# Attention of sorted blocks and a feed-forward layer: transposes on the DMA queues or on TensorE, and a product that gives x^T directly

## The chip, the cores and the metric

The kernel runs on one core of one Trainium2 chip. The metric is the device time of one execution in microseconds (us), as the median of several runs. The engines are TensorE (PE, with its weight loads as PEld), VectorE (DVE), ScalarE (ACT), GpSimd (POOL) and SyncE (SP), which here only issues transfers; POOL issues the loads. Each engine takes its instructions in order, and engines wait for each other by semaphores.

## The reference, cut to what matters

```python
q, k, v: (4, 8, 768, 64)   sort_net: (4, 8, 8, 8)   block = 96
P = sort_net                                    # Sinkhorn, 5 rounds
for _ in range(5):
    P = exp(P - max(P)); P = P / sum(P, -1); P = P / sum(P, -2)
k_sorted = einsum('bhij,bhjcd->bhicd', P, k in 8 blocks of 96)
v_sorted = einsum('bhij,bhjcd->bhicd', P, v in 8 blocks of 96)
scores = (q @ k_sorted^T) / 8                   # inside each block of 96
attn = exp(scores - max); attn = attn / sum(attn, -1)
x = attn @ v_sorted                             # to (3072 tokens, 512)
out = relu(x @ w_in) ** 2 @ w_out               # 512 -> 2048 -> 512, float32
```

## The kernel before

**Work.** The four batches are b = 0 to 3. A *unit* is a pair of heads (hp = 0 to 3) of one batch; a *half* (hf) is four of its eight blocks, 384 positions. The feed-forward layer is worked in eight FFN units of 384 tokens: unit g belongs to batch g // 2, half g % 2. An FFN unit needs `xT` (attention's result, features on partitions) of all four head pairs of its half. It is 16 *ups* (four matmuls of 384 columns each, L997), each followed by a ReLU on ACT (L1005) and a square on DVE (L1008), and then three tiles of 128 tokens in four *down* quarters each (four matmuls of 512 columns, L1027); a tile's result is copied by ACT and written out by SP.

**Attention of one unit.** k and v are sorted: blocks are mixed with weights from P. Batch 0 does it with `w_all` (P times a mask, `s_sort`, L613, and `s_sort2`, L649), which leaves k^T and v^T; `s_vt` (L733) turns v back. Later batches load k and v with four rows of a block in one partition row and sort them with the small `w_t` in 32x32 parts of the array (`s_nat`, L769), which leaves them untransposed; v goes out to HBM and back to come block by block (`v_way`, `vblk`). Two units of batch 1 sort k by `s_sort`. `s_q` (L563) turns q on PE for those and for batch 0. The other ten units take `s_turn`: natural k (`kn`) and a paired copy of q (`qi`, made by DVE, L841) are each turned by a transposing transfer issued by SP, and DVE puts k^T in block order (L829). `s_sc` makes the scores (L684) and ACT their exponentials `et`. In `s_av` a matmul with `et` stationary and v moving (65 columns, the last of ones) gives x and the sums (L875); DVE takes reciprocals of the sums (96x8, L885) and multiplies (L886) into `ao`. `s_xt` turns `ao` into `xT`: by a transposing transfer for eleven whole units and three single halves of batch 0, and by PE (L928) for the rest.

**Buffers.** Scores, later sorts and `attn v` share two PSUM buffers `p2` (ring `r2`). Ups and downs share three (`pf`, ring `rf`), the ReLUs' outputs `h1` have three, output tiles four. `ps1` has one.

**Order.** Everything is first entered in a `Plan`: each operation with an engine, a price in us, what it depends on. FFN work and attention work are two queues for PE; `DUES` says after how many FFN pieces an attention stage is due, and `FIRST` gives the order of the first batch's first halves. `Plan.run` plays this through with its prices and emits each engine's instructions in the resulting order, which is fixed from then on; where PE would have idled early, `fill` puts matmuls with `ones`. Loads of batches 2 and 3 wait for a POOL copy (`held`) that reads `xT` of the batch before; a gate on POOL holds one load of batch 1 back.

Of the kernel before, what the change touches and what calls it, by code (L numbers as in the profile page):

```python
# [11 lines left out]
ALU = mybir.AluOpType  # L12
# [9 lines left out]
    (0, "K"): (-265.0, -237.0, -495.0, -419.0),  # L22
    (0, "S"): (-232.5, -234.0, -349.0, -310.0),
    (0, "T"): (-184.0, -236.0, -400.0, -291.5),
    (0, "A"): (-135.0, -150.0, -300.0, -111.0),
    (0, "X"): (-58.0, -109.0, -251.5, -80.5),
    (0, "W"): (-267.0,),
    (1, "V"): (-117.0, -62.5),
    (1, "Q"): (-58.5,),
    (1, "N"): (None, -31.0),  # L30
    (1, "Z"): (None, None, 2.5, 48.5),
    (1, "S"): (-45.5, -5.0, 5.0, 50.0),
    (1, "A"): (-27.0, -4.5, 31.5, 51.5),
    (1, "X"): (40.0, 23.5, 37.0, 53.5),
    (2, "L"): (40.0,),
    (2, "N"): (75.5, 79.0),
    (2, "V"): (60.5, 82.5),
    (2, "Z"): (81.0, 82.5, 94.0, 83.5),
    (2, "S"): (86.0, 86.5, 96.0, 93.5),
    (2, "A"): (86.0, 88.0, 99.0, 94.5),  # L40
    (2, "X"): (97.5, 103.0, 103.0, 102.0),
    (3, "L"): (109.0,),
    (3, "N"): (111.5, 130.0),
    (3, "V"): (112.5, 144.0),
    (3, "Z"): (128.5, 139.0, 153.0, 149.0),
    (3, "S"): (144.0, 153.0, 158.0, 153.5),
    (3, "A"): (145.0, 153.5, 159.5, 154.5),
    (3, "X"): (150.5, 170.0, 236.5, 211.5),
# [4 lines left out]
FIRST = ("K0' v0 K1 v1 S0 t0' S1 t1' A0 K2' V2 A1 K3 S2 t2 v3 S3 x1' A2 T3' x0' A3 X2' F0 F1 F3 "  # L53
         "F4 F6 F7 X3")
# [130 lines left out]
def kernel(  # L185
# [48 lines left out]
    rkx, rkn, rqi, rqz = Ring(3), Ring(4), Ring(4), Ring(6)  # L234
# [43 lines left out]
    kvT_r, et_r, vs_r, qz_r = [], [], [], []  # L278
    for n in range(3):
        sT = const.tile([128, 2, S + 32], BF16, name=f"kvT{n}")  # L280
        for x in (HS, S):
            nc.vector.memset(sT[:, :, x:x + 32], 0.0)
        kvT_r.append(sT)
        qz = const.tile([128, 2, NA, 128], BF16, name=f"qz{n}")
        qz_r.append(qz)
        vs = (qz.rearrange("p h a x -> p (h a x)")[0:96, 0:NB * 2 * 66]
              .rearrange("p (n h x) -> p n h x", n=NB, h=2))
        nc.vector.memset(vs[:, :, :, D:D + 1], 1.0)
        vs_r.append(vs)
# [11 lines left out]
    kn_r = [const.tile([128, NA, 2, D], BF16, name=f"kn{n}") for n in range(4)]  # L301
    qi_r = [const.tile([128, NA, 2, D], BF16, name=f"qi{n}") for n in range(4)]
    kx_r = []
    for n in range(3):
        kx_r.append(const.tile([128, 128 * NA], BF16, name=f"kx{n}"))
# [8 lines left out]
    w_all = const.tile([128, H + HP, NB, C0], BF16)  # L314
# [22 lines left out]
    def in_tiles(b, t, h0):  # L337
        return b > 1 and t > 0 or b == 1 and t == 2 or b == 1 and t == 1 and h0 == HP
# [44 lines left out]
    def loads_after(deps):  # L383
# [5 lines left out]
        def gate(e):  # L389
            nc.gpsimd.tensor_copy(out=xT[0:1, 0:HP - 1, HS:HS + 1],  # L390
                                  in_=w_out_bf[0:1, NT // 2 - HP + 1:NT // 2, 0:1])

        for t, g in ((2, 0), (2, 1), (1, 0), (0, 0), (1, 1), (0, 1)):
            if t == 0 and g == 1:
                holds["gate"] = plan.add("POOL", 0.1, gate, [landed["w_out", 1]])
                deps = [holds["gate"]]
            load(1, t, HP * g, HP, deps=deps)
            if t == 2 and g == 1:
                landed["last"] = plan.add("DMA", 1.5, lambda e: None, [landed["last"]])
# [131 lines left out]
    class Unit:  # L531


        def __init__(self, b, hp, halves):
            self.b, self.hp, self.halves = b, hp, halves
            self.tiled = in_tiles(b, 1, HP * (hp // 2))
            self.n, self.old = rks.take()
            if self.tiled:
                self.ksT = kvT_r[self.n][:, 0, :]
                self.i0, self.ni, self.full = 0, NB, True  # L540
                return
# [126 lines left out]
    def s_sc(u, due=0):  # L668
# [3 lines left out]
        for hf in u.halves:  # L672
# [4 lines left out]
            def mm(e, hf=hf, st=st, slot=slot):  # L677
                st["p"] = scp = p2[slot]
                if not u.tiled:
                    qT = (tiles["qT", u.b, u.hp].rearrange("p a x -> p (a x)")  # L680
                          .rearrange("p (i q) -> p i q", q=BLK))
                for n in range(NQ):
                    for h in range(2):
# [3 lines left out]
                            rhs=(q_late(u.qz)[64 * h:64 * (h + 1), :,  # L687
                                              C0 * (NQ * hf + n):C0 * (NQ * hf + n + 1)]
                                 if u.tiled else qT[64 * h:64 * (h + 1), NQ * hf + n, :]),
# [5 lines left out]
            if u.tiled:  # L695
                rqz.use(u.qz, pe)
            else:
                rqT.use(qTs[u.b, u.hp], pe)
# [52 lines left out]
    k_nat = {}  # L751

    def s_nat(b, g, t, due):

        if t == 2:
            m, oldm = rvn.take()
        evs = []
        for hp in (2 * g, 2 * g + 1):
            slot, old = r2.take()
            if t == 1:  # L760
                m, oldm = rkn.take()
# [13 lines left out]
            def ev(e, hp=hp, slot=slot, m=m):  # L775
                dst = (vn_r[m][:, :, 2 * (hp % 2):2 * (hp % 2) + 2, 0:D] if t == 2
                       else kn_r[m])
                copy(e, dst, p2[slot][:, :, 0:NA * D].rearrange("p e (a d) -> p a e d", d=D))
# [7 lines left out]
            if t == 1:  # L786
                rkn.use(m, op)
                k_nat[b, hp] = m, op
        if t == 1:
            return  # L790

# [22 lines left out]
    def q_late(z):  # L814
        return qz_r[z % 3][:, z // 3, :, :]

    def s_turn(u):

        b, hp = u.b, u.hp
        m, op = k_nat[b, hp]  # L820
        kx, oldx = rkx.take()

        def k_turn(e):
            nc.sync.dma_start_transpose(
                out=kx_r[kx].rearrange("p (a x) -> p a x", a=NA),
                in_=kn_r[m].rearrange("p a e d -> p (a e d)"))

        def k_blocks(e):
            nc.vector.tensor_copy(out=u.ksT[:, 0:S].rearrange("p (n x) -> p n x", n=NB),  # L829
                                  in_=kx_r[kx].rearrange("p (x n) -> p n x", n=NB))  # L830

        sp = plan.add("SP", 1.4, k_turn, [op, loaded(b)] + oldx)
        k_op = plan.add("WAY", 1.3, lambda e: None, [sp])
        rkn.use(m, k_op)
        u.k_op = plan.add("DVE", 0.87, k_blocks, [k_op] + u.old)
        rkx.use(kx, k_op, u.k_op)

        n, oldi = rqi.take()

        def q_pair(e):  # L840
            nc.vector.tensor_copy(  # L841
                out=qi_r[n].rearrange("p a e d -> p e a d"),
                in_=qkv[b][0][:, 2 * hp:2 * hp + 2, :].rearrange("p e (a d) -> p e a d", d=D))

        qp = plan.add("DVE", 0.4, q_pair, [landed[b, 0, HP * (2 * hp // HP), 0]] + oldi)
        readers[b].append(qp)
        rqi.use(n, qp)
        u.qz, oldz = rqz.take()

        def q_turn(e):  # L850
            nc.sync.dma_start_transpose(
                out=q_late(u.qz), in_=qi_r[n].rearrange("p a e d -> p (a e d)"))

        sp = plan.add("SP", 1.4, q_turn, [qp, loaded(b)] + oldz + [op for ops in rvs.all for op in ops])
# [350 lines left out]
```

## Time and profile before

| what | value |
|---|---|
| median of 3 runs (lowest, highest) | 217.92 us (217.73, 217.99) |
| profiled execution, its own time | 217.95 us |
| span of the profiled execution | 216.2 us |
| PE busy | 209.8 us (97%) |
| DVE, ACT, POOL busy | 109.2, 122.1, 28.3 us |
| granted PE clock | 1.00 |
| ups and downs on PE (L997, L1027) | 506 and 352 matmuls recorded |
| transposing transfers (`xT<-ao`, `kx<-kn`, `qz<-qi`) | 14, 10, 10; median 3.6, 3.9, 3.6 us to landing |
| DMA queues, share of 16 engines | q1 (SP) 40.1%, q0 (POOL) 36.9% |

The span runs from the first to the last instruction; the rest of the execution's own time lies around it. A row such as `L885 DVE RECIPROCAL rec<-p 96x8 f32<-96x8 f32 x32 | busy, mean ns | idle before` names a line of the kernel, its engine and operation, the tiles written and read with partitions x elements, how many there were, their time in all and each, and how long the engine sat idle just before them and for whom. The chain that ended last is followed back from the last instruction, at each step to what released it. Matmuls are pipelined, so a mean of one is longer than the distance from one start to the next.

### The profile page before, as it was taken

The page shows a single profiled execution, that of the slowest core. Times are in us where ns is not written, and L with a number is a line of the kernel's source. Part 1 is how long each engine was busy: PE and PEld are TensorE (multiplying, and loading weights), DVE is VectorE, ACT ScalarE, POOL GpSimd, SP SyncE. Part 2 cuts the span into 40 slices and gives each one's busy share as a digit, 9 for nine tenths or more (in the row PEclk, how much of TensorE's full clock was granted, in tenths as well). Part 3 has the DMA queues.
Part 4 walks back from the last instruction along what each step waited for, and adds up shares of the span by engine and source line. Part 5 has one row for each costly group of instructions (what it writes and reads, how often), then busy time and mean ns, then how long its engine had stood idle before and what let it go on. Part 6 is the DMA issues. An engine that isn't in the chain of part 4 may idle for free.

```text
span 216.2 us, 5062 instructions
## 1 busy us (share of the span) xinstructions
PE 209.8 (97%) x2020; PEld 115.9 (54%) x2036; DVE 109.2 (51%) x297; ACT 122.1 (56%) x251; POOL 28.3 (13%) x53
## 2 busy tenths in 40 slices
PE   8998999999999999999999999999999999999994
PEld 2566675446654565445655455445655465455542
DVE  5777677146795446345875047407775154015300
ACT  4876985248765277347774178318874375137421
POOL 7896230000000700000000420000000000000000
PEclk9999999999999999999999999999999999999999
DMA  6999999999978599199995699497978410120012
GB/s 152 212 203 207 207 207 209 193 226 272 176 164 113 84 238 211 25 192 210 179 186 125 105 201 213 87 207 171 170 204 111 102 47 3 49 97 0 0 52 97
DMA packets 47864, 31.92 MB, mean 148 GB/s; under 512 B 27296, under 2 KB 42912, under 8 KB 47840
## 3 DMA queue, kind: packets, MB, share of 16 engines
q1 hardware_dynamic: 35616, 18.35, 40.1%
q0 software_dynamic: 12224, 13.24, 36.9%
q8 instruction: 16, 0.26, 0.5%
q14 instruction: 8, 0.07, 0.1%
HBM read 29.70 MB, written 8.72 MB: 178 GB/s over the span
## 4 chain that ended last, share of the span: by engine, by line
PE 93%; DVE 2%; ACT 2%; issue 1%; DVEq 0%
PE hp L997 37%; PE op L1027 36%; PE p L875 4%; PE p L440 4%; PE p L684 3%; PE p L769 2%; PE op L1055 2%; PE qtp L563 2%; DVE ao L886 1%; PE vbp L733 1%; PE p L649 1%; DVE h L1008 1%; ACT h L1005 1%; PE xtp L928 1%; PE hp L955 0%
## 5 line engine op out<-in xcount | busy, mean ns | idle before, releaser
L997 PE MATMUL hp<-xT,w_in_bf 128*128 128x384 bf16 x506 | 87.6, 326 | 0.0
L1027 PE MATMUL op<-w_out_bf,h 128*128 128x512 bf16 x352 | 83.3, 379 | 0.9 <-issue 0.2
L1008 DVE TENSOR_TENSOR h<-h 128x384 bf16<-128x384 bf16 x128 | 43.9, 355 | 56.2 <-ACT h L1005 55.7
L1005 ACT ACTIVATE h<-hp 128x384 bf16<-128x384 f32 x128 | 61.7, 495 | 17.7 <-PE hp L997 14.9
L997 PEld LDWEIGHTS <-w_in_bf 128*128 128x128 bf16 x506 | 47.7, 98 | 32.2 <-issue 1.1
L1027 PEld LDWEIGHTS <-h 128*128 128x128 bf16 x368 | 33.9, 98 | 37.9 <-issue 1.0
L248 ACT COPY ob<-op 128x512 f32<-128x512 f32 (+2 forms) x25 | 14.2, 568 | 49.1 <-PE op L1027 46.6
L713 ACT ACTIVATE et<-p 96x384 bf16<-96x384 f32 x48 | 19.9, 488 | 6.4 <-PE p L684 6.4
L886 DVE TENSOR_TENSOR ao<-p,rec 96x512 bf16<-96x512 f32 x32 | 22.0, 686 | 1.1
L875 PEld LDWEIGHTS <-et 96*128 96x128 bf16 x256 | 11.2, 97 | 5.5 <-issue 0.7
L885 DVE RECIPROCAL rec<-p 96x8 f32<-96x8 f32 x32 | 6.4, 201 | 11.1 <-PE p L875 10.5
L1144 POOL COPY held<-xT 1x3 bf16<-1x3 bf16 (+1 forms) x2 | 0.4, 183 | 85.0 <-DMA xT<-ao 85.0
L440 PE MATMUL p<-ones 128*128 128x512 bf16 (+1 forms) x28 | 9.2, 460 | 1.1 <-DVE ones L274 1.1
L875 PE MATMUL p<-vblk,et 96*128 96x65 bf16 x192 | 9.4, 193 | 0.1
L250 DVE CAST vn<-p 128x768 bf16<-128x768 f32 x6 | 5.7, 958 | 7.3 <-PE p L769 7.2
L250 DVE CAST kn<-p 128x768 bf16<-128x768 f32 x5 | 4.8, 958 | 9.1 <-PE p L769 9.1
L684 PEld LDWEIGHTS <-kvT 64*128 64x128 bf16 x256 | 6.2, 94 | 5.5 <-issue 3.6
L829 DVE COPY kvT<-kx 128x768 bf16<-128x768 bf16 x10 | 8.5, 850 | 0.0
L248 ACT CAST vn<-p 128x768 bf16<-128x768 f32 x6 | 4.8, 798 | 5.8 <-PE p L769 5.8
L324 POOL DMA_DIRECT2D kb<-in_k_dram x10 | 6.5, 648 | 4.1 <-DMA w_in_bf<-in_moe_w_in_dram 2.0
L248 ACT CAST kn<-p 128x768 bf16<-128x768 f32 x5 | 4.0, 806 | 4.7 <-PE p L769 4.7
L324 POOL DMA_DIRECT2D vb<-in_v_dram x10 | 6.3, 633 | 2.3 <-DMA w_in_bf<-in_moe_w_in_dram 2.1
(81 smaller groups left out, 118.8 us busy)
## 6 DMA issues: line engine op xcount, KB each, us to landing
out_dram<-ob SPq DMA_DIRECT2D x23, 256.0 KB, 3.4
v_way<-vn SPq DMA_DIRECT2D x6, 396.0 KB, 5.1
vblk<-v_way SPq DMA_DIRECT2D x6, 396.0 KB, 4.3
vb<-in_v_dram POOLq DMA_DIRECT2D x6, 384.0 KB, 11.7
kb<-in_k_dram POOLq DMA_DIRECT2D x6, 384.0 KB, 10.4
qb<-in_q_dram POOLq DMA_DIRECT2D x6, 384.0 KB, 13.1
w_in_bf<-in_moe_w_in_dram POOLq DMA_DIRECT2D x4, 512.0 KB, 10.4
w_out_bf<-in_moe_w_out_dram POOLq DMA_DIRECT2D x4, 512.0 KB, 15.7
```

Of the source, the lines that this page charges most:

```text
L248: nc.scalar.copy(out=out, in_=in_)
L250: nc.vector.tensor_copy(out=out, in_=in_)
L324: nc.gpsimd.dma_start(out=dst, in_=src)
L440: nc.tensor.matmul(out=p2[slot][:, 0, 0:128 * r].rearrange("p (r x) -> p r x", r=r), lhsT=ones, rhs=ones[:, None, :].to_broadcast([128, r, ...
L684: nc.tensor.matmul(out=scp[:, h, BLK * n:BLK * (n + 1)], lhsT=u.ksT[64 * h:64 * (h + 1), HS * hf + BLK * n:HS * hf + BLK * n + 128], rhs=( ...
L713: nc.scalar.activation(out=et[:, h, 0:HS].rearrange("p (n c a) -> p n c a", c=C0, a=NA), in_=st["p"][0:96, h, 0:HS].rearrange("p (n a c) - ...
L875: nc.tensor.matmul(out=oup[:, h, 66 * n:66 * n + D + 1], lhsT=et_r[u.et[hf]][:, h, BLK * n:BLK * n + 128], rhs=(u.vs[:, NQ * hf + n, h, 0: ...
L886: nc.vector.tensor_tensor(out=u.ao[:, n0:n0 + NQ, :, :].rearrange("p n e d -> p e n d"), in0=ov[:, :, :, 0:D], in1=rec[:, :, :, None].to_b ...
L997: nc.tensor.matmul(out=t["hp", nt][:, 0:HS], lhsT=w_in_bf[:, kc, 128 * nt:128 * (nt + 1)], rhs=xT[:, kc, t0:t0 + HS], start=(kc == 0), sto ...
L1005: nc.scalar.activation(out=t["h1", nt], in_=t["hp", nt][:, 0:HS], func=AF.Relu)
L1008: nc.vector.tensor_tensor(out=t["h2"][:, nt, :], in0=t["h1", nt], in1=t["h1", nt], op=ALU.mult)
L1027: nc.tensor.matmul(out=t["op", mt], lhsT=t["h2"][:, nt, 128 * mt:128 * (mt + 1)], rhs=w_out_bf[:, nt, :], start=(nt == 0), stop=(nt == NT ...
```

## The change

No transposing transfer is left. All later units sort k by `s_sort` with `w_all` on PE (L587 in the new numbering) and turn q by `s_q` on PE (L537), each now a stage of its own in `DUES` ("J" and "Q"). For batches 1 to 3, and for the second half of batch 0, `s_av` hands over to `s_av_t`: v is stationary and `et` moving, so that the product comes out as x^T with the two heads on two halves of the partitions; the sums over the keys come from a second product with `ones` stationary, in the second bank of the same `p2` buffer, and are the same on each of a head's 64 partitions. DVE then takes reciprocals of 192 columns on 128 partitions (L799, twice per half) and multiplies straight into `xT` (L803, twice per half). `w_all` is built for all heads, for batches 2 and 3 by POOL. The loads keep their order, but k is loaded in the layout of batch 0 in every batch. The gate is gone, and `held` waits for the second half.

```diff
 DUES = {
...
-    (3, "N"): (111.5, 130.0),
-    (3, "V"): (112.5, 144.0),
-    (3, "Z"): (128.5, 139.0, 153.0, 149.0),
-    (3, "S"): (144.0, 153.0, 158.0, 153.5),
-    (3, "A"): (145.0, 153.5, 159.5, 154.5),
-    (3, "X"): (150.5, 170.0, 236.5, 211.5),
...
+    (3, "V"): (112.5, 123.0),
+    (3, "S"): (122.5, 149.0, 150.0, 142.0),
+    (3, "A"): (124.5, 157.0, 166.5, 146.5),
...
+    (3, "Q"): (114.0, 118.0, 125.5, 125.5),
+    (3, "J"): (115.0, 145.5, 126.0, 139.5),
 }
...
-FIRST = ("K0' v0 K1 v1 S0 t0' S1 t1' A0 K2' V2 A1 K3 S2 t2 v3 S3 x1' A2 T3' x0' A3 X2' F0 F1 F3 "
-         "F4 F6 F7 X3")
+FIRST = ("k0 V0 v1' K1 S0 t0' k2 S1 v2 K3 A0 T1' V3 t2 S2 A1 T3' A2 x0' S3 x1' X2' A3 F1 F0 F4 "
+         "F6 F7 F3 X3")
...
-    w_all = const.tile([128, H + HP, NB, C0], BF16)
+    w_all = const.tile([128, NH, NB, C0], BF16)
...
-        return b > 1 and t > 0 or b == 1 and t == 2 or b == 1 and t == 1 and h0 == HP
+        return b > 0 and t == 2
...
-        def gate(e):
-            nc.gpsimd.tensor_copy(out=xT[0:1, 0:HP - 1, HS:HS + 1],
-                                  in_=w_out_bf[0:1, NT // 2 - HP + 1:NT // 2, 0:1])
...
-    def s_turn(u):
...
-            nc.sync.dma_start_transpose(
-                out=kx_r[kx].rearrange("p (a x) -> p a x", a=NA),
-                in_=kn_r[m].rearrange("p a e d -> p (a e d)"))
...
-            nc.sync.dma_start_transpose(
-                out=q_late(u.qz), in_=qi_r[n].rearrange("p a e d -> p (a e d)"))
...
+    rrec, parts = Ring(4), {}
+
+    def s_av_t(u, due=0):
+
         if u.b > 0:
             w, u.vs_op = v_blk[u.b, u.hp // 2]
+        for hf in u.halves:
+            slot, old = r2.take()
+
+            def mm(e, hf=hf, slot=slot):
+                et = et_r[u.et[hf]]
+                for h in range(2):
+                    nc.tensor.matmul(
+                        out=p2[slot][64 * h:64 * (h + 1), 1, 0:HS],
+                        lhsT=ones[0:96, 0:D], rhs=et[:, h, 0:HS], start=True, stop=True)
+                for n in range(NQ):
+                    for h in range(2):
+                        nc.tensor.matmul(
+                            out=p2[slot][64 * h:64 * (h + 1), 0, BLK * n:BLK * (n + 1)],
+                            lhsT=(u.vs[:, NQ * hf + n, h, 0:D] if u.b < 1 else
+                                  vb_r[w][:, NQ * hf + n, 2 * (u.hp % 2) + h, 0:D]),
+                            rhs=et[:, h, BLK * n:BLK * (n + 1)], start=True, stop=True)
+
+            pe = plan.add("PE", 0.34, mm, u.exps[hf] + [u.vs_op] + old, due, mode="col")
+            r2.use(slot, pe)
+            for c in (slice(0, HS // 2), slice(HS // 2, HS)):
+                st = {}
+
+                def inv(e, c=c, slot=slot, st=st):
+                    st["r"] = att.tile([128, HS // 2], FP32, tag="rec_t", name="rec_t", bufs=4)
+                    nc.vector.reciprocal(out=st["r"], in_=p2[slot][:, 1, c])
+
+                def norm(e, hf=hf, c=c, slot=slot, st=st):
+                    t0 = S * u.b + HS * hf + c.start
+                    nc.vector.tensor_tensor(out=xT[:, u.hp, t0:t0 + HS // 2],
+                                            in0=p2[slot][:, 0, c], in1=st["r"], op=ALU.mult)
+
+                so, oldr = rrec.take()
+                op = plan.add("DVE", 0.35, inv, [pe] + oldr)
+                op = plan.add("DVE", 0.36, norm, [op])
+                rrec.use(so, op)
+                r2.use(slot, op)
+                parts.setdefault((u.b, u.hp, hf), []).append(op)
+            ret.use(u.et[hf], pe)
+            if u.b < 1:
+                rvs.use(u.m, pe)
+            else:
+                rvb.use(w, pe)
+            x_done[u.b, u.hp, hf] = parts[u.b, u.hp, hf][-1]
+
+    def s_av(u, due=0):
+        if u.b > 0 or u.halves == (1,):
+            return s_av_t(u, due)
+        nao, olda = rao.take()
...
     def s_xt(u, due=0, eng=AD, own=True):
-        early = u.b == 0 and u.halves == (1,) and u.hp < HP - 1
-        if early or u.b > 1 or u.b == 1 and u.hp < HP - 1:
-            def turn(e):
-                t0 = S * u.b + BLK * u.i0
-                nc.sync.dma_start_transpose(
-                    out=xT[:, u.hp, t0:t0 + BLK * u.ni].rearrange("p (n q) -> p n q", q=BLK),
-                    in_=u.ao.rearrange("p n e d -> p (n e d)"))
...
+    def sort_k(b, hp, due):
         u = units[b, hp] = Unit(b, hp, (0, 1))
-        s_turn(u)
+        if b == 1 and hp % 2 == 0:
+            for h0 in (2 * hp, 2 * hp + 2):
+                build_w(H + h0, 2, pt, x_done[0, 2, 1])
+        u.k_op = s_sort(u, 1, due)
+        u.q_op = late_q[b, hp]
...
+    def turn_q(b, hp, due):
+        late_q[b, hp] = s_q(b, hp, 0, 128, due)
...
-        holds[b] = plan.add("POOL", 0.1, hold, [x_done[b - 1, x, 0] for x in range(HP - (b == 2))])
+        holds[b] = plan.add("POOL", 0.1, hold, [x_done[b - 1, x, 1] for x in range(HP - (b == 2))])
...
+        for h0 in range(0, H, 4):
+            build_w(H * b + h0, 4, pt, holds[b], eng="POOL")
```

## The prediction, made before the changed kernel had run

> **What bounds the kernel now.** I read the busy shares and slices first, then the chain that ended last, then the groups kept apart by shape, then the chain in order of time.
>
> ```profile
> span 216.2 us, 5062 instructions
> ...
> PE 209.8 (97%) x2020; PEld 115.9 (54%) x2036; DVE 109.2 (51%) x297; ACT 122.1 (56%) x251; POOL 28.3 (13%) x53
> ...
> PEclk9999999999999999999999999999999999999999
> ...
> PE 93%; DVE 2%; ACT 2%; issue 1%; DVEq 0%
> ```
>
> The chain is TensorE for 93% at a full clock. VectorE is half idle and nothing in the chain is a transfer: the transposing transfers are hidden. Whatever the change adds on PE is paid, and whatever it takes off the DMA queues is not earned.
>
> ```profile
> 49.24 0.67 PE p L613 x24
> ...
> 63.10 0.86 PE op L1027 x4
> 63.97 0.25 PE p L875 x8
> ...
> 64.53 0.97 PE op L1027 x4
> 65.50 0.28 PE p L684 x8
> ...
> 68.97 0.45 PE p L684 x16
> ...
> 84.03 0.31 PE p L769 x16
> ...
> 192.20 9.76 PE hp L997 x60
> ```
>
> These are pieces of the chain in time (start, length). One up-projection matmul of 384 columns takes 0.163 us. Four down matmuls take 0.86 beside `attn v` (L875, whole array) and 0.97 beside scores (L684, half array); eight score matmuls take 0.28 and sixteen 0.45. So eight are 0.17 of work, and each change between whole array and part of it costs 0.11 before and after.
>
> ```profile
> L886 DVE TENSOR_TENSOR ao<-p,rec 96x512 bf16<-96x512 f32 x32 | 22.0, 686 | 1.1
> ...
> L885 DVE RECIPROCAL rec<-p 96x8 f32<-96x8 f32 x32 | 6.4, 201 | 11.1 <-PE p L875 10.5 <-ACT kvT L248 0.3
> ...
> L250 DVE CAST kvT<-p 128x768 bf16<-128x768 f32 x3 | 2.9, 956 | 1.4 <-PE p L649 1.2
> ...
> L250 DVE CAST kvT<-tp 128x384 bf16<-128x384 f32 x3 | 1.7, 553 | 0.1
> ...
> L411 DVE TENSOR_REDUCE rs<-p_sb 32x8 f32<-32x64 f32 x5 | 1.0, 207 | 2.3 <-ACT p_sb L454 2.3
> L412 DVE RECIPROCAL rs<-rs 32x8 f32<-32x8 f32 x5 | 1.0, 191 | 0.2
> ```
>
> The two casts give VectorE's price from PSUM: (956-553)/384 = 1.05 ns a column and 150 ns fixed. A reciprocal of 8 columns should then take 158; it takes 201.
>
> **The change, TensorE.** From the instruction order of both programs. Added: 120 transposes of q and 120 sorting matmuls of k, all of 128 columns; the sort of k now costs 0.67/24 = 28 ns each, so 2 x 3.4 = 6.7 us. The product for x^T, per half of a head pair: two ones-products of 384 columns side by side (as one, 0.163) and eight of 96 columns (as the scores, 0.17) = 0.335 against 0.25 for eight of L875; 28 halves: +2.4. Removed: five natural k sorts (0.31 less a change = 0.20 each), -1.0, and 12 transposes of x at 42 ns, -0.5. Array changes rise from 93 to 128, since the x^T product is now a half-array one: 35 x 0.10 = +3.5. Sum +11.1 us, all on the chain.
>
> **Queues.** SP loses its 34 transposing transfers and the waits before them; their 1.2 to 1.3 us each hide behind nothing that PE waits for, so 0. POOL loses the gate copy and gains four `w_all` builds of twice the 0.66 us of today's 256 columns, behind the six loads of a batch; their readers, the k sorts, stand over 10 us later: 0. ACT loses five casts of k and takes seven more of the k sort, about equal (0.8 each); its 56% covers it. VectorE loses ten copies of k (0.85), ten of q (0.35), five casts (0.96) and 28 pairs L885+L886 (0.89); it gains nine evictions of q^T (0.56), two more `w_all` builds (0.42), 56 products of 192 columns (0.15 + 192 x 1.05 ns = 0.35) and 56 reciprocals of 192. The holds of batches 2 and 3 wait for the second half's normalization, a few us later than the first's; the first v sort stands 10 to 15 us behind: 0, or some us if this cover goes.
>
> **The reciprocal is the choice.** No row has a wide one. What is above 150 ns at 8 columns is either a constant (150 + 43 + 192 x 1.05 = 0.40 us) or per column: (201-150)/8 = 6.4 ns from PSUM. From SBUF the reduction of 64 columns leaves 140 fixed, and (191-140)/8 = 6.4 again. Two sources agreeing in a rate lets me take 6.5 ns a column: 0.15 + 192 x 6.5 ns = 1.40 us. The Trainium skill, VectorE: DVE Perf Modes, section "The TRN2 errata", prices any PSUM-to-SBUF operation at 120 cycles and one per column, 325 ns here; by it 8 columns would take 133, and the row says 201, so I follow the row. Another section of that page, "First, the fixed hardware budget", has the reciprocal as an iterated divide with a repeat count of 8: if that is 8 cycles a column, 1.75 us, the upper end. By 0.33 to 0.40 the sum ends at 229, by 1.40 at 267, by 1.75 near 285 (all below).
>
> **What waits for it.** The planner orders the engines for a reciprocal of 0.35 (its price in `s_av_t`). On VectorE each half is two reciprocals and two products in a row: 2 x 1.40 + 2 x 0.35 = 3.5 us (R). Each half holds one of the two score/sort buffers `p2` until its R ends, so the third product, score or sort behind two of them waits on PE, which is in order, and everything behind it waits too. Squares (L1008) queue behind R as well; ups may run six ahead of the last square (three `pf`, three `h1` buffers), 3.9 us. FFN unit 3, with A a product (0.5 with its change), D four down matmuls (0.87): the order is A A D2 A A D3 S2 D3 A A D3. First A ends at 0.3; R free the buffers at 3.9 and 7.4. PE has A A D2 done at 2.5, waits 1.4 for the third A, then 3.0 for the fourth (7.4 to 7.9), D3 to 10.5; scores wait for 10.9 (0.4) and 14.4 (3.2); D3 to 17.3; two A to 18.3; D3 to 20.9; unit 4 needs x^T of the fifth half at 21.3 (0.4). Sum 8.4. Unit 1, by the same walk: the k sort waits 1.7 and the scores 1.8 behind the first two A, then six halves with only 11 us of other work: 2.1, 1.3, 3.0, 1.5: 11.3 in all. Unit 5: k sorts 0.8 and 3.1, scores 2.1 and 1.5, products 0.4 and 3.0, unit 6's start 1.3: 12.2. Unit 2: its two halves stand right before unit 3's ups, whose squares come at 7.7; six ups and an A cover 4.4: 3.5. Unit 0: 1.5 for the squares behind a lone R and 2.7 where unit 1 needs the last two R with five D for cover: 4.2. Units 4, 6 and 7 have none. Sum 39.6.
>
> **The sum.** 216.2 + 11.1 + 39.6 - 1.0 (today's wait at 110 to 112 us, which belonged to the old normalization) = 265.9 of span. The profiled execution took 217.95, that is 1.75 outside the span, and the median is 217.92: 267.6, rounded to 267.
>
> **Rivals.** (a) The reciprocal is a constant plus one cycle a column, 0.40 us: R is 1.5 us, hidden save about 1 us behind the fourth products. 216.2 + 11.1 + 1.0 - 1.0 + 1.75 = 229. For it: the errata rule, and the planner's own price; against: the equal rate from both sources. (b) R is slow but PE finds other work: then only VectorE's sums count. Unit 1: 8 x 3.5 and 8.4 of squares and evictions = 36.4 against 30.7 of PE by the durations above; unit 5: 34.3 against 28.0; unit 3: 27.3 against 25.4. Excess 13.9, and 216.2 + 11.1 + 13.9 - 1.0 + 1.75 = 242. Against: PE's order is fixed and `p2` has two buffers. (c) Not slower: the transposing transfers and the old normalization hold PE more than the chain says, and without them the waits close up. The chain's waits that could close are 3.5 at the start (12.3 to 19.6 us), 3.9 at 108.5 to 112.4, 1.7 at the two turns of the last units: 9.1, below the 11.1 added, so 220. It decides only if the added PE work is under 9.1, for instance if array changes cost nothing beside these short products (7.6 added): 216.2 + 7.6 - 9.1 + 1.75 = 216.5. Against: 0.97 beside 0.86. (d) Loads of batches 2 and 3, now begun after later normalizations, come late: 3 to 6 us on top of the forecast, 272.
>
> **How the numbers follow.** The likeliest, slow reciprocals behind a fixed order: 0.60, its own range 250 to 285 (1.1 to 1.75 us). (a) 0.30, (b) 0.05, (c) 0.02, (d) 0.03. The range must hold (a), so it runs from 226 to 282; about a tenth of the likeliest lies above. A measurement of this kernel tells about 0.2% (0.4 us) from no change. Slower 0.97, same 0.01, faster 0.02: (c) alone gives the last two.
>
> **What would show it.** Right: the row of the 192-column reciprocal at 1.3 to 1.5 us x56; VectorE near 175 us busy; PE busy share down to some 80%; waits of PE's k sorts, scores and products for the VectorE products of `s_av_t`, in units 1, 3 and 5, each under 3.5 us. With the reciprocal at 0.4 us it is (a). The two last units stay at 20.8 us each. Wrong: a total under 222 (my PE sum fails), half-array groups whose starts are farther apart than 28 ns, a granted clock under 1.0 in the waiting stretches (not counted), or PE waiting for transfers.

## The result, and the profile after

| | before | changed |
|---|---|---|
| median of 4 runs each, side by side (us) | 217.95 (217.73 to 218.43) | 268.45 (267.74 to 269.42) |
| ratio, 95% interval | | 1.2316 (1.2269 to 1.2363) |
| span of the profiled execution | 216.2 | 267.6 |
| PE busy / idle in the span | 209.8 / 6.4 | 235.2 / 32.4 |
| DVE busy | 109.2 | 161.7 |

The changed kernel is 50.5 us slower; 267 was forecast. In some kernels below one or two executions were disturbed by the chip's state; they are left out of the times, and such an execution is used only for the profile of the kernel with 96 columns, for VectorE's durations alone. These are the lines of the changed kernel's page that answer to those shown of before: span and busy shares, PE and clock by slices, the chain by engine.

```profile
span 267.6 us, 5448 instructions
...
PE 235.2 (88%) x2241; PEld 126.3 (47%) x2241; DVE 161.7 (60%) x336; ACT 129.0 (48%) x258; POOL 34.0 (13%) x56
...
PE   8799899897875999996995899999877959999995
...
PEclk9999999999997799999798999999979898999999
...
PE 63%; DVE 27%; ACT 4%; issue 2%; DMA 2%; SPq 0%; DVEq 0%; ACTq 0%
```

TensorE has fallen from 97% to 88% busy, VectorE is in 27% of the chain where it was in 2%, and the clock row, flat before, has gaps. The transfers are still no part of it: 2%, nearly all of it the first loads. The groups by shape say which VectorE operation it is (busy, mean ns, idle before and for whom):

```profile
L799 DVE RECIPROCAL rec_t<-p 128x192 f32<-128x192 f32 x56 | 71.8, 1324 | 20.7 <-PE p L786 20.7
L803 DVE TENSOR_TENSOR xT<-p,rec_t 128x192 bf16<-128x192 f32 x56 | 15.6, 320 | 0.0
```

The reciprocal takes 1.324 us and the product after it 0.320, so a half costs R = 2 x 1.324 + 2 x 0.320 = 3.29 us. Who waits is in the view of waits, PE's part and one line of ACT's (us in all, times, longest):

```profile
PE p L781 <- DVE xT L803: 8.5, 6, 2.5
PE p L657 <- DVE xT L803: 7.4, 5, 2.4
PE p L587 <- DVE xT L803: 4.4, 3, 2.3
PE hp L939 <- ACT h L947: 3.4, 3, 2.7
PE hp L939 <- DVE xT L803: 1.2, 1, 1.2
...
ACT h L947 <- DVE h L950: 9.3, 6, 3.5
```

The x^T products (L781), scores (L657) and k sorts (L587) all wait for the products `xT` of `s_av_t`, that is, for one of the two `p2` buffers; ups (L939) wait for ReLUs (L947), and ReLUs wait in turn for squares (L950) queued behind an R. No wait of PE is over 2.7 us. The chain in order of time, in FFN unit 3, shows the walk of the prediction:

```profile
137.30 0.28 PE p L781 x2
...
139.14 1.29 DVE rec_t L799
...
140.91 2.48 DVE rec_t L799 x2
...
143.85 0.26 DVE h L950
144.12 2.48 DVE rec_t L799 x2
...
147.07 2.47 DVE rec_t L799 x2
...
150.07 0.34 PE p L657 x8
```

Products first, then four R back to back on VectorE with one square slipped in (L950), then the score that waited for the buffer. The same stretch in PE's timeline, and twelve downs a little later (start, length, in brackets the wait before):

```profile
137.23 0.35 PE L781 MATMUL p<-et,ones 96*64 96x384 bf16 x2
...
137.59 0.33 PE L781 MATMUL p<-et,ones 96*64 96x384 bf16 x2
...
140.96 0.36 PE L781 MATMUL p<-et,ones 96*64 96x384 bf16 x2 [1.04 <-DVE xT L803]
...
143.91 0.35 PE L781 MATMUL p<-et,ones 96*64 96x384 bf16 x2 [2.42 <-DVE xT L803]
...
144.36 4.45 PE L969 MATMUL op<-w_out_bf,h 128*128 128x512 bf16 x12
...
153.83 2.76 PE L969 MATMUL op<-w_out_bf,h 128*128 128x512 bf16 x12
```

The third and fourth product wait 1.0 and 2.4 us for an R (1.4 and 3.0 were forecast). Then comes what was not forecast: twelve down matmuls take 4.45 us where the twelve at 153.83 take 2.76. TensorE is at half clock here, as the view by windows shows for two neighbouring stretches at the start of the same FFN unit (stretch, length, busy time and count of PE, PEld, DVE, ACT and POOL, then granted clock, DMA share, GB/s):

```profile
124.20:127.60 3.40, 0.99 (x7) 0.59 (x7) 3.27 (x9) 1.40 (x4) 0.00 (x0) 1.00 0.00 0
...
127.60:131.00 3.40, 3.40 (x12) 1.66 (x11) 1.19 (x4) 1.33 (x3) 0.00 (x0) 0.50 0.00 0
```

In the 3.4 us before, PE was busy for 0.99; in the 3.4 us after, it has work all the time and the clock is 0.50. There are six such half-clock stretches, one of 6.8 us and five of about 3.4; the same view adds them up:

```profile
sum 24.00, PE 23.08 PEld 9.63 DVE 16.27 ACT 7.31 POOL 2.60; mean PE 3.85 PEld 1.60 DVE 2.71 ACT 1.22 POOL 0.43
```

Of these 24.0 us PE is busy for 23.08. At full clock the work would have taken about half (in the chain eight downs take 3.53 at 84.6 us and 1.83 at 112.6), so some 11.5 us of PE busy time is due to the clock.

### The profile page after: what moved, and what is told of

The parts are those of the page before. It is cut to its first block, busy times and chain, and to the rows that moved or that the text cites. A ratio compares the mean times of both kernels' runs of the same rounds, so it can differ in the third digit from the quotient of the medians.

```text
span 267.6 us, 5448 instructions
## 1 busy us (share of the span) xinstructions
PE 235.2 (88%) x2241; PEld 126.3 (47%) x2241; DVE 161.7 (60%) x336; ACT 129.0 (48%) x258; POOL 34.0 (13%) x56
## 2 busy tenths in 40 slices
DMA packets 23737, 25.54 MB, mean 95 GB/s; under 512 B 1248, under 2 KB 19424, under 8 KB 23712
## 4 chain that ended last, share of the span: by engine, by line
PE 63%; DVE 27%; ACT 4%; issue 2%; DMA 2%; SPq 0%; DVEq 0%; ACTq 0%
PE op L969 25%; PE hp L939 24%; DVE rec_t L799 20%; DVE xT L803 4%; PE qtp L537 2%; DVE h L950 2%; PE p L657 2%; DMA xT<-in_q_dram 2%; ACT h L947 2%; PE p L587 2%; PE p L781 1%; PE op L997 1%; PE p L419 1%; PE p L786 1%; ACT et L672 1%
## 5 line engine op out<-in xcount | busy, mean ns | idle before, releaser
L939 PE MATMUL hp<-xT,w_in_bf 128*128 128x384 bf16 x506 | 90.7, 335 | 4.7 <-ACT h L947 3.4
L969 PE MATMUL op<-w_out_bf,h 128*128 128x512 bf16 x368 | 91.6, 400 | 0.6 <-ACT h L947 0.6
L799 DVE RECIPROCAL rec_t<-p 128x192 f32<-128x192 f32 x56 | 71.8, 1324 | 20.7 <-PE p L786 20.7
L947 ACT ACTIVATE h<-hp 128x384 bf16<-128x384 f32 x128 | 61.4, 491 | 32.6 <-PE hp L939 22.1
L950 DVE TENSOR_TENSOR h<-h 128x384 bf16<-128x384 bf16 x128 | 47.8, 383 | 44.8 <-ACT h L947 44.1
L939 PEld LDWEIGHTS <-w_in_bf 128*128 128x128 bf16 x506 | 49.2, 100 | 40.6 <-issue 10.1
L242 ACT COPY ob<-op 128x512 f32<-128x512 f32 (+2 forms) x25 | 14.2, 568 | 63.3 <-PE op L969 60.9
L781 PE MATMUL p<-et,ones 96*64 96x384 bf16 x56 | 9.8, 345 | 8.5 <-DVE xT L803 8.5
L657 PE MATMUL p<-qT,kvT 64*128 64x96 bf16 x256 | 10.0, 211 | 7.6 <-DVE xT L803 7.4
L803 DVE TENSOR_TENSOR xT<-p,rec_t 128x192 bf16<-128x192 f32 x56 | 15.6, 320 | 0.0
L242 ACT CAST kvT<-p 128x768 bf16<-128x768 f32 x13 | 10.4, 800 | 8.0 <-PE p L587 7.7
L657 PEld LDWEIGHTS <-kvT 64*128 64x128 bf16 x256 | 6.9, 98 | 13.6 <-issue 11.4
L244 DVE COPY qT<-qtp 128x768 bf16<-128x768 bf16 x11 | 6.1, 556 | 10.8 <-PE qtp L537 10.8
L781 PEld LDWEIGHTS <-ones 96*64 96x64 bf16 x56 | 3.8, 108 | 14.5 <-issue 14.3
L537 PE MATMUL qtp<-ident,qb 128*64 128x128 bf16 (+1 forms) x240 | 8.9, 212 | 1.3 <-ACT qb L439 1.2
L587 PE MATMUL p<-w_all,kb 128*64 128x128 bf16 x144 | 6.1, 226 | 4.4 <-DVE xT L803 4.4
L537 PEld LDWEIGHTS <-qb 128*64 128x64 bf16 (+1 forms) x240 | 6.4, 109 | 6.8 <-issue 4.2
## 6 DMA issues: line engine op xcount, KB each, us to landing
qb<-in_q_dram POOLq DMA_DIRECT2D x6, 384.0 KB, 12.5
w_out_bf<-in_moe_w_out_dram POOLq DMA_DIRECT2D x4, 512.0 KB, 16.2
```

The costliest lines, as they stand in the source:

```text
L242: nc.scalar.copy(out=out, in_=in_)
L244: nc.vector.tensor_copy(out=out, in_=in_)
L537: nc.tensor.transpose(out=t["p"][64 * h:64 * (h + 1), a, :], in_=qb[p0:p1, 2 * hp + h, D * a:D * (a + 1)], identity=ident[p0:p1, p0:p1])
L657: nc.tensor.matmul(out=scp[:, h, BLK * n:BLK * (n + 1)], lhsT=u.ksT[64 * h:64 * (h + 1), HS * hf + BLK * n:HS * hf + BLK * n + 128], rhs=q ...
L781: nc.tensor.matmul(out=p2[slot][64 * h:64 * (h + 1), 1, 0:HS], lhsT=ones[0:96, 0:D], rhs=et[:, h, 0:HS], start=True, stop=True)
L799: nc.vector.reciprocal(out=st["r"], in_=p2[slot][:, 1, c])
```

## The experiments

**The reciprocal by itself.** A kernel that runs only reciprocals and copies of several widths from PSUM and SBUF, and writes zeros as output.

> The reciprocal by itself on VectorE: 8, 32, 96, 192 and 384 columns of fp32 on 128 partitions, three of each, from PSUM and from SBUF, and copies of the same sizes; 192 and 384 columns from bf16. The rest of the computation is left out and zeros are written. Theory (a price per column): 192 columns 1.3 us, 384 columns about 2.5 us, 96 about 0.74, a slope of 6.1 to 6.4 ns a column from both memories, where the copies have 1.05. Rival (a constant once it is wide, or waiting for the PSUM port beside ScalarE and TensorE in the full kernel): alone, 192 columns take 0.35 to 0.45 us.

Groups by shape of this kernel (`src_p` in PSUM, `src_s` in SBUF, `half` bfloat16 in SBUF):

```profile
L41 DVE RECIPROCAL dst<-src_p 128x384 f32<-128x384 f32 x3 | 7.7, 2557 | 0.1
...
L41 DVE RECIPROCAL dst<-src_p 128x192 f32<-128x192 f32 x3 | 4.1, 1357 | 0.1
L41 DVE RECIPROCAL dst<-src_s 128x192 f32<-128x192 f32 x3 | 4.1, 1353 | 0.1
L49 DVE RECIPROCAL dst<-half 128x192 f32<-128x192 bf16 x3 | 4.1, 1353 | 0.1
...
L44 DVE COPY dst<-src_p 128x384 f32<-128x384 f32 x3 | 1.7, 557 | 0.1
...
L44 DVE COPY dst<-src_p 128x192 f32<-128x192 f32 x3 | 1.1, 357 | 0.1
```

(2557 - 1357)/192 = 6.25 ns a column for the reciprocal, (557 - 357)/192 = 1.04 for the copy: six times as much, and the same from either memory and from either type. The price belongs to the operation; neither of these places or types for its input would help.

**A copy in place of each reciprocal.** Everything else, the order included, is the changed kernel's; the division by the sums is left out.

```diff
-                    nc.vector.reciprocal(out=st["r"], in_=p2[slot][:, 1, c])
+                    nc.vector.tensor_copy(out=st["r"], in_=p2[slot][:, 1, c])
```

> The changed kernel with the reciprocals of 192 columns replaced by copies of the same shape from the same place, so the division is left out; every instruction else and its order stay. Theory (the reciprocal's duration makes the waits): the copy takes 0.35 us, four operations of a half 1.4 us, the waits of PE for VectorE go from 25 us to about 1, the granted clock stays at 1.0, and the time is the PE sum alone, 216.2 + 11.1 + 1.75 = 229 us. Rival (the new PE work, its array changes or the later loads cost more than summed): over 240 us.

229.89 and 230.92 us, before beside it 217.70. Its copies, and PE's longest wait for another engine's work after the start-up:

```profile
L799 DVE COPY rec_t<-p 128x192 f32<-128x192 f32 x56 | 17.3, 350 | 23.0 <-PE p L786 22.9
```

```profile
PE hp L939 <- ACT h L947: 0.4, 1, 0.4
```

All waits for `xT` are gone and PE is busy for 96%. So the added TensorE work is worth 12.2 to 13.2 us, and the price of the reciprocals 38 of the 50.5. This is also the forecast's rival (a) built by hand, and its 229 holds. Laid beside the changed kernel, FFN unit by FFN unit (from the first up of a unit to the first of the next, from the windows of the three kernels), it shows where those 38 us fall:

| FFN unit | before | with copies | changed | changed - copies | waits forecast |
|---|---|---|---|---|---|
| 0 | 27.30 | 27.70 | 29.90 | 2.2 | 4.2 |
| 1 | 28.10 | 31.02 | 42.99 | 12.0 | 11.3 |
| 2 | 22.42 | 26.22 | 26.22 | 0.0 | 3.5 |
| 3 | 25.89 | 25.49 | 36.55 | 11.1 | 8.4 |
| 4 | 22.01 | 24.27 | 24.82 | 0.6 | 0 |
| 5 | 25.54 | 28.23 | 40.74 | 12.5 | 12.2 |
| 6 | 20.76 | 20.76 | 21.33 | 0.6 | 0 |

With what lies before unit 0 (0.7) the differences come to the 39.5 us between the two spans, 267.6 and 228.1.

**Half as many columns.** Reciprocals of 96 columns, each used for both of its blocks; half of the divisors are left out.

```diff
-                    nc.vector.reciprocal(out=st["r"], in_=p2[slot][:, 1, c])
+                    nc.vector.reciprocal(out=st["r"][:, 0:BLK],
+                                         in_=p2[slot][:, 1, c.start:c.start + BLK])
...
+                        in1=st["r"][:, None, 0:BLK].to_broadcast([128, 2, BLK]), op=ALU.mult)
```

> The changed kernel with reciprocals of 96 columns instead of 192, each used for both of its blocks, so half of the division is left out; number and order of the instructions stay. Theory (a price per column): 0.74 us each, a half takes 2.1 us of VectorE instead of 3.3, and most of the waits close: 233 to 243 us. Rival (a price per instruction): the reciprocal stays near 1.3 us and the time near 268.

237.8 us, ratio 1.0900 (1.0867 to 1.0934).

```profile
L799 DVE RECIPROCAL rec_t<-p 128x96 f32<-128x96 f32 x56 | 38.2, 723 | 18.9 <-PE p L786 18.9
```

The price is paid per column, but the kernel's time does not follow it in proportion. R is 2 x 0.350 + 2 x 0.347 = 1.39 with copies, 2 x 0.723 + 2 x 0.319 = 2.08 here and 3.29 in the changed kernel. The first step adds 28 x 0.69 = 19 us of VectorE work and about 7 us of time; the second adds 28 x 1.21 = 34 and 31 of time. Of the first step about a third is on the path, of the second nine tenths; part of the second is the clock's, which was 1.00 in the executions counted here and is 0.955 in the changed kernel's profile. Where between these three values of R the slope changes was not measured.

**The planner told the true price.** Is the order, made for a reciprocal of 0.35 us, to blame?

```diff
-                op = plan.add("DVE", 0.35, inv, [pe] + oldr)
+                op = plan.add("DVE", 1.33, inv, [pe] + oldr)
```

> The changed kernel with the planner's price of the reciprocal at 1.33 instead of 0.35, nothing else: the same instructions in another fixed order. Theory (two p2 buffers held for 3.3 us each and VectorE's own sum bind, whatever the order): a part comes back, 250 to 262 us. Rival (the order made for the wrong price is the whole wait): about 240 us, VectorE's sums alone.

267.69 us, ratio 1.2315 (1.2251 to 1.2379): no gain, outside what either theory gave. PE's waits and the clock by slices of this kernel:

```profile
PE p L657 <- DVE xT L803: 11.5, 5, 2.6
PE p L781 <- DVE xT L803: 8.6, 5, 2.4
```

```profile
PEclk9999999999595999999995799999999856999999
```

PE's waits for `xT` are 21.4 us, as in the changed kernel (21.5): they only changed places, and the clock fell further (0.928 against 0.955 on the mean). With two buffers and an in-order VectorE the planner, knowing the price, found no place for the R either.

**The buffers given back early.** ACT copies the whole half (768 columns) out of `p2`; VectorE works on the copy.

```diff
+            def away(e, slot=slot, xs=xs):
+                xs["t"] = att.tile([128, 2, HS], FP32, tag="xs", name="xs", bufs=4)
+                nc.scalar.copy(out=xs["t"], in_=p2[slot][:, :, 0:HS])
...
+            aw = plan.add("ACT", cost_f(2 * HS)[0], away, [pe] + oldx)
+            r2.use(slot, aw)
...
-                    nc.vector.reciprocal(out=st["r"], in_=p2[slot][:, 1, c])
+                    nc.vector.reciprocal(out=st["r"], in_=xs["t"][:, 1, c])
```

> The changed kernel, but ScalarE first copies sums and product of each half out of the p2 buffer (768 columns, 0.8 us, into one of four tiles), and VectorE's reciprocals and products read the copy: the buffer is free after 0.8 us instead of 3.3. VectorE's work and order stay. Theory (the two buffers pass VectorE's delay on to PE): the 20 us in which PE waits for VectorE's products before a score, sort or product fall to a few; VectorE's own sum still holds up squares and the start of units 2, 4, 6: 240 to 252 us. Rival (VectorE in order is the whole bind and the delay only moves to the squares): 260 us or more.

258.7 us, ratio 1.1879 (1.1813 to 1.1946): between the two expectations. All waits for `p2` behind VectorE are gone, and another has come:

```profile
PE hp L948 <- DVE xT L812: 12.4, 4, 3.9
PE hp L948 <- ACT h L956: 3.8, 3, 3.0
```

Ups now wait for x^T itself and for ReLUs whose buffers wait for squares behind the R. Freeing the buffers is worth about 10 us, net of the copies that ACT makes for it. Of the 28.8 us of span that this kernel still has above the one with copies for reciprocals (256.9 and 228.1), the two waits shown, both behind VectorE's queue, are 16.2; part of the rest is the clock (0.967), and it was not split further.

**Both of these together**: early buffers and the price of 1.33.

> ScalarE copies the halves out of p2 as before, and the planner also has the reciprocal at its real price, 1.33. Theory (VectorE's sums bind once the buffers are free, and the order can then be made for them): 240 to 250 us. Rival (the order in which one in-order VectorE serves squares and reciprocals has no better place: the right price alone changed nothing): 255 to 262 us, as without the price.

286.78 us, ratio 1.3160 (1.3079 to 1.3240), outside what either theory gave. The wait and a piece of the chain in order of time:

```profile
PE hp L948 <- ACT h L956: 39.7, 6, 14.9
```

```profile
70.13 2.52 DVE rec_t L808 x2
...
84.91 2.47 DVE rec_t L808 x2
...
89.08 0.28 DVE h L959
```

From 70.1 to 89.1 us VectorE does six R in a row, while the squares of the next ups stand behind them and PE, out of `h1` and `pf` buffers, waits for up to 14.9 us. But six R in a row are found with early buffers alone too (74.3 to 91.5 us). PE's timeline there, and then in this kernel:

```profile
79.77 5.35 PE L978 MATMUL op<-w_out_bf,h 128*128 128x512 bf16 x24
...
89.13 6.08 PE L948 MATMUL hp<-xT,w_in_bf 128*128 128x384 bf16 x19 [3.52 <-DVE xT L812]
```

```profile
89.92 2.40 PE L948 MATMUL hp<-xT,w_in_bf 128*128 128x384 bf16 x7 [14.91 <-ACT h L956]
```

With early buffers alone the six R stand beside downs, which need nothing of VectorE, and PE waits 3.5 us. With the true price as well they stand among ups, whose squares share VectorE's queue with them. Why the planner chose so was not looked into; a true price does not by itself make a good order.

**The q, k half alone** (on the kernel before): no transposing transfers of q and k, sorts and turns on PE, x as before.

```diff
-        s_turn(u)
+        if b == 1 and hp % 2 == 0:
+            for h0 in (2 * hp, 2 * hp + 2):
+                build_w(H + h0, 2, pt, x_done[0, 2, 1])
+        u.q_op = s_q(b, hp, 0, 128, due)
+        u.k_op = s_sort(u, 1, due)
```

> The half with q and k alone, built on the kernel before: q turned and k sorted by TensorE for the ten later units, at the places in the order where the transfers had been issued; x, its small reciprocals and its transposing transfers stay as they were. In the earlier try a stage stood ahead of its loads in the queue of attention work, and PE waited 7.7 us for q. Theory (this half costs PE work only): 6.7 - 1.0 + 19 array changes more at 0.10 = 7.6, so 225 us, no wait of PE for loads, clock 1.0. Rival (this half has waits of its own): over 232 us.

(The earlier try is the kernel "q and k on PE, x by transfers" below.)

225.92 us, ratio 1.0371 (1.0343 to 1.0399), +8.2 at a full clock. PE busy is 217.0, that is +7.2, and no wait of PE is over 1.1 us. The transfers given up on SP's queue brought nothing.

**The x^T half alone** (on the kernel before, batches 1 to 3), and the same with copies (the division left out).

```diff
+        if u.b > 0:
+            return s_av_t(u, due)
```

> The other half alone: the kernel before, with the x^T product, wide reciprocals and no turning of x for batches 1 to 3; q and k stay with the transposing transfers. Theory (the reciprocals make the loss): 2.0 us for the products, 30 array changes more at 0.10, and waits of 30 to 40 us in FFN units 1, 2, 3 and 5, clock under 0.97: 252 to 263 us. Rival: the waits need the k sorts and turned q on the same two buffers, and are small without them: 225 to 240 us.

257.21 us, ratio 1.1803 (1.1715 to 1.1892), as expected. The reciprocals of this kernel, and its largest wait:

```profile
L886 DVE RECIPROCAL rec_t<-p 128x192 f32<-128x192 f32 x48 | 61.5, 1325 | 7.1 <-PE p L873 5.6 <-ACT et L710 1.1 <-ACT h L1054 0.3
```

```profile
PE p L681 <- DVE xT L890: 19.8, 14, 2.6
```

> The x^T product alone on the kernel before, with the reciprocals replaced by copies of the same shape (the division is left out). Theory (beside the reciprocals this half costs PE work only): 24 halves at 0.085 = 2.0, less 0.3 for eight turned blocks, 30 array changes more at 0.10: 222.4 us. Against the same kernel with reciprocals (257 us) that puts some 35 us on the reciprocals, without the q and k half. Rival (the x^T product itself waits, on its two buffers): over 230 us.

225.7 us, ratio 1.0352 (1.0314 to 1.0390), some 3 us above what was expected. PE's waits past the start-up:

```profile
PE p L681 <- ACT et L710: 1.2, 2, 0.8
...
PE p L868 <- ACT et L710: 0.8, 2, 0.4
```

Scores and products wait 2.0 us for exponentials, at 160 to 163 us, and a half-clock stretch follows in the profiled execution (its clock 0.991). PE is busy for 217.9 us, 8.1 more than before. A v block that lands at 113.46 us (in both of these kernels the hold on a batch's loads waits for the second half) holds PE up by 0.3 us only. How the 3 us split between work and these waits stays open. Between these two kernels only the operation differs: 31 us for 48 reciprocals, with q and k still turned by transfers (the clock is part of it: 0.94 to 0.96 against 0.99 to 1.00). The reciprocals need no help from the q, k half to cost what they cost.

**q and k on PE, x by transfers** (from the changed kernel, with my own due times for the transfers of x).

```diff
-        if u.b > 0 or u.halves == (1,):
+        if u.halves == (1,):
             return s_av_t(u, due)
```

> One half of the change alone: q and k of batches 1 to 3 are turned and sorted by TensorE as in the changed kernel, but x of those batches is made as before (sums of 8 columns, transposing transfers); the second half of batch 0 keeps the x^T product. Theory (this half costs PE work only): 6.7 us of q and k, less 1.0 of natural k sorts, 23 array changes more at 0.10, 2.6 us in FFN unit 0 as seen in the changed kernel: 217.7 + 10.6 = 228 us, VectorE near 100 us busy, clock 1.0. Rival (half of the loss comes from this side, by its order or its later loads): over 240 us.

247.04 us, ratio 1.1356 (1.1288 to 1.1423), 19 us above what was expected, and no evidence on the question. PE's waits show another cause:

```profile
PE qtp L540 <- DMA qb<-in_q_dram: 7.7, 1, 7.7
PE hp L961 <- DMA xT<-ao: 3.9, 2, 2.4
```

A q turn stood in PE's order ahead of its load; most likely because x, later by its transfer, opened the hold on the loads later. The q, k half on the kernel before, above, took its place.

**The clock.** The changed kernel with idle matmuls with `ones` in front of the products and scores that wait longest, to keep PE busy.

```diff
+    keep = {("A", 9): 1.5, ("S", 15): 2.0, ("A", 18): 2.0, ("S", 24): 0.8, ("S", 29): 1.5, ("A", 28): 2.1}
...
+        n = int(keep.get((stage, seen[stage]), 0) / 0.216)
```

> The changed kernel with 0.8 to 2.1 us of idle matmuls with ones, into the spare ps1 buffer, ahead of six products and scores that waited 1.2 to 2.7 us (the 9th, 18th and 28th product, the 15th, 24th and 29th group of scores): PE is busy where it waited. Theory (the waits also let the clock fall to half, and PE then works at half rate for some us on the path; in the profile eight down matmuls took 3.5 us instead of 1.7): the granted clock rises from 0.955 to 0.98 or more and 3 to 6 us come back, 262 to 265 us. Rival (the half clock lies in stretches that VectorE bounds anyway): 267 to 269 us, the same.

263.45, 267.04 and 267.10 us, ratio 1.2199 (1.2111 to 1.2288). The clock rose to 0.993, 0.980 and 0.979 where the changed kernel had 0.948 to 0.959, but only the first run is in the range of the theory. The filled waits gave 1 to 5 us, and the interval of the ratio overlaps the changed kernel's (1.2269 to 1.2363); how much the clock costs in all is not settled by this.

**The division on ACT**, as exp(-ln(sum)), VectorE left with the product.

```diff
+                nc.scalar.activation(out=st["r"], in_=p2[slot][:, 1, 0:HS], func=AF.Ln)
...
+                nc.scalar.activation(out=st["r"], in_=st["r"], func=AF.Exp, scale=-1.0)
```

> The changed kernel with the division moved to ScalarE: the logarithm of 384 sums and then exp of its negative, in place of the two reciprocals of a half; VectorE keeps the two products. The compiled order has 38 activation-table loads more, since logarithm and exponential lie in different tables; one took 1.28 us in the profile of before. Theory (it is the time that a half holds its p2 buffer and its in-order engine, on whichever engine): ScalarE gets 28 x 2 x 0.49 + 38 x 1.28 = 76 us more, 2.7 us per half, about what VectorE had in reciprocals, and the ReLUs stand behind it: 250 to 270 us. Rival (only VectorE's reciprocal matters, ScalarE has the room): under 240 us, near the 230 of the copies.

277.9 us, ratio 1.2724 (1.2695 to 1.2753), worse than either expectation. ACT's groups:

```profile
L798 ACT ACT_TABLE_LOAD x19 | 24.4, 1283 | 0.9 <-DVE xT L809 0.6
L801 ACT ACT_TABLE_LOAD x19 | 24.4, 1283 | 0.3
L801 ACT ACTIVATE rec_t<-rec_t 128x384 f32<-128x384 f32 x28 | 13.6, 517 | 0.2
L798 ACT ACTIVATE rec_t<-p 128x384 f32<-128x384 f32 x28 | 12.8, 489 | 0.2
```

The two functions themselves take 1.0 us a half against 2.65 for the reciprocals, but each change of function between them loads a table at 1.283 us, 48.8 us in all, on an engine whose ReLUs the ups wait for. VectorE is down to 98.9 us and the kernel is slower all the same.

No version that was run beats the kernel before: even with the division at the price of a copy the change adds 12 us.

## Why the prediction was right

**The bound and the worthless relief** were right. PE bounded before, the transfers were hidden, and taking q's and k's off the queue earned nothing (+8.2 with them gone).

**TensorE +11.1.** The sum held: measured as +12.2 to +13.2 with the reciprocals' price out of the way, of which up to 1 was the wait that rival (a) allowed. The pieces: 24 sorting matmuls still take 0.67 (54.86 us in the chain), and in the timeline above one product starts 0.36 after the other where the forecast had 0.335. The whole-array neighbour again pays: four downs take 0.97 beside scores in this chain too.

**The reciprocal.** 1.40 was forecast from 8 columns and a rate of 6.5 ns; it is 1.324. The choice of a price per column over a constant held. That the rate came out within 4% was in part luck: it stands on a rest of 51 ns over 8 columns (201 - 150), so 10 ns of error in the fixed part would have moved 192 columns by 0.24 us. The lone kernel has the fixed part at 157 ns from PSUM and 153 from SBUF (1357 and 1353, each less 192 x 6.25), where 150 and 140 were used, and its copies from SBUF cost 0.52 ns a column ((360 - 260)/192), not the 1.05 behind the 140. With 157 and 153 the same two rows would have given 5.5 and 4.8 ns, and not one rate. Both estimates from the Trainium skill's page "VectorE: DVE Perf Modes" missed: the formula in "The TRN2 errata" gives 325 ns, a quarter of what was measured, and the reading of eight cycles a column from "First, the fixed hardware budget" gives 1.75 us; the measured slope, six times the copy's, lies between.

**The waits, 39.6.** (Two small slips: unit 1's terms add up to 11.4, not 11.3, and unit 2's, 7.7 less 4.4, to 3.3, not 3.5. The 285 us for a reciprocal of 1.75 is not worked out.) The changed kernel is 39.5 us of span longer than the one with copies, in the units that were named: 14.2 in units 0 and 1 (15.5 forecast), 11.1 in units 2 and 3 (11.9), 12.5 in unit 5 (12.2), about 1 in units 4 and 6. Unit 2's wait is found at unit 3's first ups, which begins the next row of the table.

**But not all of that 39.5 is waiting**, and here the agreement is luck in good part. PE's idle time rises only by 23.9 (from 228.1 - 219.6 = 8.5 to 32.4); its busy time rises by 15.6. The term that was mis-sized is the walk through the waits, 39.6 where some 24 to 26 us were waited: R was 3.29 and not 3.5, and some 41 reciprocals, 20 R, lie on the chain (20% of 267.6 us by 1.324), so about 4 us; single waits came out at 2.4 where 3.0 was forecast. The term that was left out is the clock, named in the prediction as not counted. It accounts for some 11.5 of the 15.6; the page of the kernel with copies also has 20 matmul records fewer (2221 against 2241), so its busy time is a little low (its view of waits has 1.9 us of gaps before downs with no releaser). Not all of the 11.5 is on the path either: in the stretch at 144.36 above the next score waits for an R anyhow. Adding up only the slowed pieces that lie on the chain (84.6, 126.6, 196.6, 205.9 and 219.2 us: 19.5 us where the same matmuls take 11.7 at full clock) gives about 8. So waits put too high and a clock put at nothing made up for each other.

**The signs.** The reciprocal's row and the waits, where they were named and under 3.5 us, came as forecast. VectorE busy came to 161.7 and not near 175, PE's share to 88% and not some 80% (its own numbers give (209.8 + 11.1)/265.9 = 83%), the two last units to 21.3 and 21.1 us and not 20.8. And one sign that it had listed as of being wrong came: a granted clock under 1.0 in the waiting stretches.

**The rivals.** (a) was the other large case and its number, 229, is what the copies gave. (b), that PE finds other work and only VectorE's sums count, would have been 242; neither the planner with the true price nor early buffers reached it. Its sums were also too high: VectorE is busy for 32.6, 26.3 and 27.4 us in units 1, 3 and 5 (windows), not 36.4, 27.3 and 34.3. Since PE needs 30.5, 25.1 and 27.8 in the same units with copies, a better order could in principle hide much of R; no order that does was found, and that stays open. (c) falls with +8.2 for half of the change. (d) did not come: DMA holds 2% of the chain. A late load did appear in one experiment that mixed old and new parts (7.7 us for q).

The sentence "PE's order is fixed and `p2` has two buffers" was right and too short. The experiments show three couplings: the buffers (10 us when freed), the squares in VectorE's queue (the worst case, 286.8, where six R stood among ups), and the clock.

## What to carry to other kernels

Before an operation is widened, get its price per column from two rows of different width or memory, and multiply: a rate that is hidden in a fixed cost at 8 columns is nearly the whole price at 192. Two wide rows of the operation alone leave no room for luck (6.25 ns a column here). A long operation on an in-order engine is paid by whoever needs its buffer or stands behind it in its queue, and the part of it that is on the path grows with its length (here a third of the VectorE time added between 1.4 and 2.1 us a half, nine tenths of that added between 2.1 and 3.3). It is best put beside work that does not need its engine: six R beside downs cost PE a wait of 3.5 us, six among ups 14.9. A queue that is hidden returns nothing when it is relieved, so a change that spends the bound engine's time on it needs a gain elsewhere.

## What the hardware showed that was not expected

Waits of at most 2.7 us were enough to halve TensorE's clock. The Trainium skill, "TensorE: Matmul & The Clock Gate", section "HAM oscillation — how this bites in real kernels", has as its rule that there be no idle gap above about 3.4 us; no gap here was that long, so the measurement goes further than the rule. In the 3.4 us ahead of the six half-clock stretches PE was busy for 1.30, 0.99, 0.98, 0.58, 1.61 and 1.01 us, always under half; a stretch with 1.62 (76.4 to 79.8 us) was not followed by one. The traces of all kernels here that run the computation, taken together, say more. In each of them the clock falls and returns at times that lie a whole number of 3.41 us apart. Cut at these times, they have 26 stretches at full clock in which PE was busy for under 1.5 us, and each was followed by half clock; of 810 with over 1.8 us one was (2.09 us, in the kernel with early buffers and true price), and of the 16 between, six. It looks as if the share of work in such a stretch decides, but no run varied that share alone.

The reciprocal's rate is the same for bfloat16 and float32 and for PSUM and SBUF, where a copy of 192 columns takes 357 ns from PSUM and 260 from SBUF.
